# A threshold-attention and hardswish kernel on Trainium2: a different order of loads, warm-ups, biases and scores in its first microseconds, and a last tile in two halves

## The chip, the cores and the metric

The kernel runs on one core of one Trainium2 chip. The metric is the device time of one execution in microseconds (us). Only this core is used, so nothing is exchanged with other cores. In the tables, PE is the matmul engine, PEld its weight load, DVE the vector engine, ACT the scalar engine, POOL GpSimd, and SP the engine that issues most of the DMAs; a q behind a name stands for the engine's instruction queue.

## The reference, cut to what matters

The inputs are q, k and v of shape (8, 8, 576, 64), that is 8 batches of 8 heads, and the weights w_in (512 x 2048) and w_out (2048 x 512).

```python
scores = scale * np.matmul(q, k.transpose(0, 1, 3, 2))            # scale = 1/8
thresh = np.max(scores, axis=-1, keepdims=True) - tau             # tau = 0.02
scores = np.where(scores >= thresh, scores, -1000000000.0)
attn = softmax(scores)                       # with 1e-9 added to the sum
x = np.matmul(attn, v)                       # 4608 tokens x 512
h = x @ w_in
g = h * np.clip(h + 3.0, 0.0, 6.0) / 6.0
out = g @ w_out                              # 4608 x 512, float32
```

So each row of scores needs its maximum before anything else can be done to it. What lies under the maximum less tau is thrown away, the rest goes through a softmax, is multiplied by v, and the result of all heads goes through two large matmuls with a hardswish between them.

## The kernel before

**Work units.** A pair is two heads that share one tile of 128 rows: head a = 0 in rows 0 to 63, a = 1 in rows 64 to 127. A quad is two pairs, so there are 16 quads. A quad has 9 slots: 4 slots for each pair, of 128 queries each for both heads, and a ninth slot for the last 64 queries of both pairs. There are 144 slots. The main loop runs over them, with n as the slot's number. It is written for in-order engines: the order of the statements is the order on each engine, and no scheduler moves anything (`manual_schedule`).

**A slot's way.** `scores(n)` (L278) multiplies q and k on PE, in float32, into PSUM. A head's scores are 576 columns, more than a bank of 512, so each head takes two banks and two matmul calls, a wide and a narrow one. `sm_max` (L295) copies a head's scores to SBUF on DVE and takes the maximum in the same pass. `sm_bias` (L307) makes tau - scale * maximum on POOL. `sm_mask` (L310) on ACT adds that bias and blows up what is below zero; `sm_exp` (L315) on ACT takes the exponential and the sum. `sm_recip` (DVE) and `sm_norm` (POOL) normalise into bf16. Then the probabilities are transposed, by PE (`pe_transpose`, L336) or by a DMA from SP's queue (L333), and `av_main` and `av_rest` multiply them with v. `mm1`, `mm1_relu`, `mm1_gate` and `mm2_part` are the two large matmuls, from slot N1 = 22 on.

**Where the scores lie.** `score_col` (L275) puts head a = 1 in banks 0 and 1 and head a = 0 in banks 3 and 4, for every slot up to 24. Banks 2 and 5 take turns for transposes and products (`bank`), banks HB = 6 and OB = 7 serve the large matmuls later. At the start bank 6 holds the output of warm-ups, which nobody reads, and banks 6 and 7 hold the first transposes (`lead`).

**The lead-in.** `load_quad(0)` issues the loads of the first quad: `load_k(n)` and `load_q(n)` for pair n, two DMAs of 128 KB each, and `rest`, four DMAs of 32 KB for the last 64 keys (kr) and queries. SP issues them in the order k of pair 0, rest, k of pair 1, q of pair 1; the two DMAs for q of pair 0 are on ACT's queue. Meanwhile PE does `warm_up(17)`, transposes of an identity matrix that POOL makes first, so that PE is working when the data come. Then PE transposes the keys (L233) and, after 4 more warm-ups, the queries and kr (L461 to L466). ACT and DVE copy these out of PSUM (`evict`, L469 to L472), the first copy of keys on ACT since `copy_out` (L219) takes DVE for 0 <= now <= N1 and ACT otherwise. `scores(0)`, `sm_max`, `sm_bias` and `scores(1)` follow, and the loop begins. In slot n < N0 = 3 the loop does, in this order: the exponentials of slot n - 1 and the maxima and bias of slot n + 1, `sm_recip`, the masks of slot n, the transposes of `turns` with their copies, warm-ups, `scores(n + 2)` and six more warm-ups, `sm_norm`, and one or more loads. `turns` says which slot transposes which part of q and k: for quad 0, q of pair 1 in slot 1, k of pair 1 in slot 2, the rest of q in slot 3.

**The middle.** The rest of quad 3's k is transposed in slot 22 and copied at the start of slot 23 by `copy_out`, on ACT. For quads of batches 0 and 1 (quads 0 to 3) SP issues `rest`; for later quads POOL does, and k's part alone. Quad 4's is issued around slot 20.

**The end.** After the loop `rest2` works off what is left of the second matmul, in tiles of 128 tokens x 512 columns, 16 matmuls of 512 columns to a tile. `mm2_out` scales a tile on ACT or DVE into one of three buffers (osb), and `flush` sends it from SP. The very last tile (`last_out`, L656) is split: ACT evicts its left half and sends it on its own queue, DVE its right half, which SP sends.

Of the kernel before, what the change touches and what calls it, by code (L numbers as in the profile page):

```python
# [9 lines left out]
F32 = mybir.dt.float32  # L10
BF16 = mybir.dt.bfloat16
Ax = mybir.AxisListType
Alu = mybir.AluOpType
Act = mybir.ActivationFunctionType

P = 128
# [4 lines left out]
def kernel(  # L21
# [10 lines left out]
    nc = tc.nc  # L32
# [50 lines left out]
    def load_quad(quad):  # L83
        b, g = divmod(quad, 2)
        nat[quad] = (nat_pool.tile([P, 1152], F32, tag="nq", name="nq"),
                     nat_pool.tile([P, 4, 4, D], F32, tag="km", name="km"),
                     nat_pool.tile([P, 2 * D], F32, tag="kr", name="kr"))
        nq, km, kr = nat[quad]

        def main(dst, src, h, order, by=nc.sync):  # L90
            by.dma_start(out=dst[:, :, h, :], in_=src[b, 4 * g + h, 0:512, :].rearrange(order, t=4))

        def blocks_q(n, a, j):
            c = 32 * (2 * a + j)
            nc.sync.dma_start(out=nq[c:c + 32, n * S:(n + 1) * S].rearrange("p (k d) -> p k d", d=32),
                              in_=q[b, 4 * g + 2 * n + a, :, 32 * j:32 * j + 32].rearrange("(k r) d -> r k d", r=32))

        def blocks_k(n, a, j):
            c = 32 * (2 * a + j)
            nc.sync.dma_start(  # L100
                out=km[c:c + 32].rearrange("p t h d -> p (t h d)")[:, n * 512:(n + 1) * 512].rearrange(
                    "p (t m d) -> p t m d", t=4, d=32),
                in_=k[b, 4 * g + 2 * n + a, 0:512, 32 * j:32 * j + 32].rearrange("(m r t) d -> r t m d", r=32, t=4))

        def load_k(n):
            if b < NB:
                for a in range(2):
                    main(km, k, 2 * n + a, "(p t) d -> p t d")
            else:
                for a in range(2):  # L110
                    for j in range(2):
                        blocks_k(n, a, j)

        def load_q(n):
            if b < NB:
                for a in range(2):
                    main(nq[:, 0:1024].rearrange("p (t h d) -> p t h d", h=4, t=4), q, 2 * n + a, "(t p) d -> p t d",
                         by=nc.scalar if quad == n == 0 else nc.sync)
            else:
                for a in range(2):  # L120
                    for j in range(2):
                        blocks_q(n, a, j)

        def rest():
            for dst, src in ((kr[:], k), (nq[:, 1024:1152], q))[0:2 if b < NB else 1]:
                for n in range(2):
                    (nc.sync if b < NB else nc.gpsimd).dma_start(out=dst[64 * n:64 * n + 64, :].rearrange("p (h d) -> p h d", h=2),
                                      in_=src[b, 4 * g + 2 * n:4 * g + 2 * n + 2, 512:S, :].rearrange("h p d -> p h d"))

        def both():  # L130
            rest()
            load_k(1)

        if b < NB:
            loads.extend((lambda: load_k(0), lambda: load_q(0), rest, lambda: load_k(1), lambda: load_q(1)))
        else:
            loads.extend((lambda: load_q(0), lambda: load_k(0), lambda: load_q(1), both))
# [47 lines left out]
        for _ in range(count):  # L185
            nc.tensor.transpose(ps[:, HB, 0:P], identf[:], identf[:])

    warm_up(17)
    identb = singles.tile([P, P], BF16)
    nc.vector.tensor_copy(out=identb[:], in_=identf[:])  # L190
    three = singles.tile([P, 1], F32)
# [25 lines left out]


    def copy_out(out, in_):  # L219
        if 0 <= now <= N1:  # L220
            nc.vector.tensor_copy(out=out, in_=in_)
        else:
            nc.scalar.copy(out=out, in_=in_)  # L223
# [46 lines left out]
        return evict  # L270

    def first(n):
        return n > N1 + 2 and n % 2

    def score_col(n, a):  # L275
        return (704 if first(n) else 128) + (0 if a else 1536)

    def scores(n):  # L278
        quad, slot = divmod(n, NSLOT)
        w0 = 320 if first(n) else 384  # L280
        for k0, w in ((0, w0), (w0, S - w0)):
            for i in range(2 if slot == 8 else 1):
                for a in range(2):
                    pair = 2 * quad + (i if slot == 8 else slot // 4)
                    rows = slice(64 * i, 64 * i + 64) if slot == 8 else slice(0, P)
                    q0 = 512 if slot == 8 else slot % 4 * P
                    c0, kc = score_col(n, a) + k0, 64 * (1 - a) + k0
                    nc.tensor.matmul(ps_flat[rows, c0:c0 + w],  # L288
                                     qT_of(pair)[a * 64:(a + 1) * 64, q0:q0 + rows.stop - rows.start],
                                     kT_of(pair)[a * 64:(a + 1) * 64, kc:kc + w], start=True, stop=True)  # L290
# [4 lines left out]
    def sm_max(sl):  # L295
# [5 lines left out]
        for i in range(2):  # L301
            c0 = score_col(sl.n, i)
            nc.vector.tensor_scalar(out=sl.s[:, i, :], in0=ps_flat[:, c0:c0 + S],  # L303
                                    scalar1=1.0, scalar2=None, op0=Alu.mult, op1=Alu.max,
                                    accum_out=sl.m[:, i:i + 1])

    def sm_bias(sl):  # L307
        nc.gpsimd.tensor_scalar(out=sl.bias[:], in0=sl.m[:], scalar1=-scale, scalar2=tau, op0=Alu.mult, op1=Alu.add)  # L308

    def sm_mask(sl, i):  # L310
        s = sl.s[:, i, :]
# [142 lines left out]

    alloc_qk(0)
    evict = transpose_k(0)
    warm_up(4)
    lead = ps[:, HB:HB + 2, :]
    q_main = nat[0][0][:, 0:1024].rearrange("p (t h d) -> p t h d", h=4, t=4)
    q_rows = bank()  # L460
# [19 lines left out]
            queue.append(sl)  # L480
    scores(0)
    sm_max(queue[0])
    sm_bias(queue[0])
    scores(1)

    turns = {1: [("q", 1)], 2: [("k", 1)], 3: [("rest", 0)]}

    def turn_at(n, job, of):
        turns.setdefault(n, []).append((job, of))
# [41 lines left out]
    for n, sl in enumerate(queue):  # L531
# [18 lines left out]
        if n + 1 < len(queue):  # L550
            if n <= N1 or n > N2 + 1 or n % 2 == 0:
                sm_max(queue[n + 1])
            sm_bias(queue[n + 1])
        even = n >= N1 and n % 2 == 0
        if n >= N0:
            sm_recip(prev)
# [70 lines left out]
            evict = []  # L627
        for out_of_psum in evict:
            out_of_psum()
        if n == 0:  # L630
            warm_up(8)
        if n < N0:
            scores(n + 2)
            warm_up(6)
# [18 lines left out]
    count = [1, 0 if todo2 and todo2[0][2] else 1]  # L653


    def last_out():  # L656
        osb = o_pool.tile([P, d_model], F32, tag="osb", name="osb")
        r0, c = B * S - 64 - P, d_model // 2
        nc.scalar.activation(out=osb[:, 0:c], in_=o_ps[0][:, 0:c], func=Act.Copy, scale=1.0 / 6.0)
        nc.scalar.dma_start(out=out[r0:r0 + P, 0:c], in_=osb[:, 0:c])  # L660
        nc.vector.tensor_scalar_mul(out=osb[:, c:2 * c], in0=o_ps[0][:, c:2 * c], scalar1=1.0 / 6.0)
        nc.sync.dma_start(out=out[r0:r0 + P, c:2 * c], in_=osb[:, c:2 * c])

    def rest1(item, then, on_act=True):
        h = mm1(item, hb=(0, 1, 3, 4)[count[0] % 4])
# [4 lines left out]
    def rest2():  # L670
        while todo2:
            bb, mt, part = todo2.pop(0)
            mm2_part(bb, mt, part, ob=OB - count[1] % 2)
            if part == 3:
                flush()
                if (bb, mt) == (B // 2 - 1, 8):
                    last_out()
                else:
                    late.extend(mm2_out(bb, mt, on_act=(count[1] % 2 == 0)))
                count[1] += 1  # L680

    av_main(2 * last + 1, 0, 256)()
# [50 lines left out]
```

## Time and profile before

| what | value |
|---|---|
| time, median of 3 runs | 516.75 us (516.36 to 516.82) |
| profiled execution, span | 515.1 us |
| PE busy | 504.9 us (98%), 4127 matmuls |
| ACT busy | 451.8 us (88%) |
| DVE busy | 441.9 us (86%) |
| POOL busy | 300.4 us (58%) |
| chain of work that ended last, by engine | PE 79%, ACT 5%, DVE 2% |

The profile is of one execution. A busy time is the sum of an engine's own instructions; waiting and issuing aren't in it. PE's instructions overlap, and their ends are modelled, so a busy PE may still be waiting a little. The chain of work that ended last is followed back from the last instruction: at each step to what released it, or to the instruction before it on its engine. In a timeline, a row gives the start, the length, the instruction and, in brackets, how long the engine had stood before it and who ended that.

### The profile page before, as it was taken

The numbers are of one execution on the slowest core, as the hardware profiler recorded it, in microseconds if no ns is written. First come the engines' busy times: TensorE is split into PE (matmuls) and PEld (weight loads), VectorE is DVE, ScalarE is ACT, GpSimd is POOL, SyncE is SP. The second block draws the span as 40 slices with busy tenths as digits, with TensorE's granted clock in tenths as the row PEclk, the third lists the DMA queues.
The fourth block names the chain that finished last, engine by engine and source line by source line (L and its number), as shares of the span: only waits on it lengthen the run. The fifth ranks groups of instructions, "written<-read, shape, count | busy, mean of one in ns | idle before, by whom it ended". The sixth has DMA issues, their size and how long they took to land.

```text
span 515.1 us, 12094 instructions
## 1 busy us (share of the span) xinstructions
PE 504.9 (98%) x4127; PEld 318.6 (62%) x4127; DVE 441.9 (86%) x1124; ACT 451.8 (88%) x980; POOL 300.4 (58%) x538
## 2 busy tenths in 40 slices
PE   8999999999999999999999999999999999999997
PEld 6655566566655666666655666666655666667563
DVE  3698898998999999999999999999999999887260
ACT  3999989999999999999999999999999999986060
POOL 0788888756666666666566756657566655552000
PEclk9999999999999999999999999999999999999999
DMA  6998999989999999999898999999999997655132
GB/s 140 163 175 140 157 148 178 160 141 176 164 195 157 173 164 170 179 176 174 164 178 143 183 169 160 159 170 168 164 173 176 183 181 114 115 111 81 74 63 61
DMA packets 314094, 78.77 MB, mean 153 GB/s; under 512 B 296624, under 2 KB 309168, under 8 KB 314032
## 3 DMA queue, kind: packets, MB, share of 16 engines
q1 hardware_dynamic: 294464, 67.90, 79.8%
q0 software_dynamic: 18368, 9.71, 15.6%
q8 instruction: 32, 0.52, 0.4%
q10 hardware_dynamic: 1200, 0.39, 0.3%
q14 instruction: 30, 0.25, 0.2%
HBM read 36.70 MB, written 9.44 MB: 90 GB/s over the span
## 4 chain that ended last, share of the span: by engine, by line
PE 79%; ACT 5%; DVE 2%; issue 0%
PE ps L288 24%; PE ps L418 24%; PE ps L384 20%; PE ps L349 7%; PE ps L379 3%; ACT s L317 2%; ACT s L312 2%; PE ps L352 1%; ACT r L392 1%; DVE g L407 1%; DVE r L394 0%; PE ps L340 0%; DVE s L303 0%; ACT kT L223 0%; PE ps L258 0%
## 5 line engine op out<-in xcount | busy, mean ns | idle before, releaser
L325 POOL TENSOR_SCALAR pn<-s,rinv 128x576 bf16<-128x576 f32 x288 | 211.4, 746 | 18.9 <-issue 4.8
L303 DVE TENSOR_SCALAR_CACHE_REDUCE s<-ps 128x576 f32<-128x576 f32 x288 | 205.0, 748 | 16.4 <-PE ps L288 8.3
L312 ACT ACTIVATE s<-s,bias 128x576 f32<-128x576 f32 x288 | 205.8, 762 | 5.1 <-POOL bias L308 4.7
L317 ACT ACTIVATE s<-s 128x576 f32<-128x576 f32 x288 | 192.4, 670 | 0.3
L288 PE MATMUL ps<-kT,qT 64*128 64x384 f32 (+7 forms) x1280 | 175.4, 419 | 3.9 <-DVE s L303 2.4
L288 PEld LDWEIGHTS ps<-kT,qT 64*128 64x128 f32 (+1 forms) x1280 | 102.9, 175 | 60.3 <-issue 15.8
L418 PE MATMUL ps<-w_out_sb,g 128*128 128x512 bf16 x576 | 134.1, 379 | 0.0
L384 PE MATMUL ps<-xT,w_in_sb 128*128 128x256 bf16 x1024 | 130.9, 273 | 0.8 <-DVE g L407 0.8
L384 PEld LDWEIGHTS <-w_in_sb 128*128 128x128 bf16 x1024 | 95.6, 98 | 40.7 <-issue 21.7
L308 POOL TENSOR_SCALAR bias<-m 128x2 f32<-128x2 f32 x144 | 27.1, 188 | 150.5 <-DVE rinv L320 135.6
L407 DVE SCALAR_TENSOR_TENSOR g<-r,ps 128x512 bf16<-128x512 f32 x128 | 87.8, 687 | 15.0 <-ACT r L392 10.8
L418 PEld LDWEIGHTS <-g 128*128 128x128 bf16 x576 | 56.2, 98 | 56.8 <-issue 0.4
L392 ACT ACTIVATE r<-ps,three 128x512 f32<-128x512 f32 x81 | 55.5, 686 | 24.7 <-PE ps L384 20.5
L317 ACT ACTIVATION_READ_ACCUMULATOR s<-s 128x1 f32 x288 | 54.4, 189 | 0.0
L394 DVE TENSOR_SCALAR r<-ps 128x512 f32<-128x512 f32 x63 | 42.9, 680 | 0.0
L349 PE MATMUL ps<-pT,vm 128*64 128x256 bf16 (+1 forms) x480 | 39.1, 285 | 0.0
L349 PEld LDWEIGHTS <-vm 128*64 128x64 bf16 x736 | 27.2, 110 | 16.1 <-issue 14.6
L360 DVE CAST xT<-ps 128x256 bf16<-128x256 f32 (+1 forms) x60 | 26.2, 436 | 10.2 <-PE ps L352 10.2
L426 DVE TENSOR_SCALAR osb<-ps 128x512 f32<-128x512 f32 x31 | 20.9, 673 | 8.4 <-PE ps L418 8.4
L303 DVE DVE_READ_ACCUMULATOR s<-ps 128x1 f32 x288 | 23.8, 83 | 0.0
L320 DVE RECIPROCAL rinv<-rsum 128x2 f32<-128x2 f32 x144 | 23.0, 159 | 0.6 <-ACT s L317 0.6
L144 POOL DMA_DIRECT2D vm<-in_v_dram x28 | 21.5, 768 | 0.7 <-issue 0.6
(57 smaller groups left out, 253.9 us busy)
## 6 DMA issues: line engine op xcount, KB each, us to landing
out_dram<-osb SPq DMA_DIRECT2D x31, 256.0 KB, 2.7
nq<-in_q_dram SPq DMA_DIRECT2D x96, 72.0 KB, 3.4
km<-in_k_dram SPq DMA_DIRECT2D x96, 64.0 KB, 3.4
vm<-in_v_dram POOLq DMA_DIRECT2D x24, 128.0 KB, 4.3
km<-in_k_dram SPq DMA_DIRECT2D x16, 128.0 KB, 4.1
w_in_sb<-in_moe_w_in_dram POOLq DMA_DIRECT2D x16, 128.0 KB, 3.6
w_out_sb<-in_moe_w_out_dram POOLq DMA_DIRECT2D x16, 128.0 KB, 4.2
pT<-pn SPq DMA_TRANSPOSE x117, 4.0
```

What stands on the lines that cost most here:

```text
L288: nc.tensor.matmul(ps_flat[rows, c0:c0 + w], qT_of(pair)[a * 64:(a + 1) * 64, q0:q0 + rows.stop - rows.start], kT_of(pair)[a * 64:(a + 1) ...
L303: nc.vector.tensor_scalar(out=sl.s[:, i, :], in0=ps_flat[:, c0:c0 + S], scalar1=1.0, scalar2=None, op0=Alu.mult, op1=Alu.max, accum_out=sl ...
L308: nc.gpsimd.tensor_scalar(out=sl.bias[:], in0=sl.m[:], scalar1=-scale, scalar2=tau, op0=Alu.mult, op1=Alu.add)
L312: nc.scalar.activation(out=s, in_=s, func=Act.Prelu, bias=sl.bias[:, i:i + 1], scale=scale, alpha=REJECT)
L317: nc.scalar.activation(out=s, in_=s, func=Act.Exp, accum_out=sl.rsum[:, i:i + 1])
L325: nc.gpsimd.tensor_scalar(out=pn[:, i, :], in0=sl.s[:, i, :], scalar1=sl.rinv[:, i:i + 1], scalar2=1.0, op0=Alu.mult, op1=Alu.mult)
L349: nc.tensor.matmul(pb[a * 64:(a + 1) * 64, :], vm[:, 2 * hp + a, c * D:(c + 1) * D], pT[:, 5 * a + c, cols], start=(c == 0), stop=False)
L384: nc.tensor.matmul(ps[:, hb, n * 256:(n + 1) * 256], w_in_sb[:, ki, (ni + n) * P:(ni + n + 1) * P], xT[b][:, ki, c0:c0 + 256], start=(ki = ...
L392: nc.scalar.activation(out=r, in_=hps, func=Act.Relu, bias=three[:])
L394: nc.vector.tensor_scalar(out=r, in0=hps, scalar1=3.0, scalar2=0.0, op0=Alu.add, op1=Alu.max)
L407: nc.vector.scalar_tensor_tensor(out=out, in0=r, scalar=6.0, in1=hps, op0=Alu.min, op1=Alu.mult)
L418: nc.tensor.matmul(o_ps[0], gbuf[:, ni, mt * P:(mt + 1) * P], w_out_sb[:, ni, :], start=(ni == 0), stop=(ni == NI - 1))
```

## The change

- **Loads of quad 0.** `load_k(0)` goes on ACT's queue and `load_q(0)` on SP's, the other way round from before. kr of quad 0 goes on ACT's queue too.
- **`rest` of quad 4.** SP issues it, not POOL (SP up to quad 4, POOL from quad 5 on).
- **Warm-ups.** Instead of 17 transposes of the identity, PE does 2 matmuls of a constant zero, which needs no identity, and 14 transposes. The 4 warm-ups before the first transposes of queries and the 8 in slot 0 go.
- **A bias per head.** For slots 0, 1 and 2 the bias of each head is made by its own POOL instruction, right after its maximum, and not one for both after the second. ACT's mask of the first head needs the first alone.
- **Scores of slots 1 and 2.** They go head by head, not wide part by wide part. In slot 1 head 0 goes into banks 6 and 7, which no slot used before, and head 1 into banks 3 and 4, where slot 0 had its head 0. In slot 2 head 0 goes into banks 0 and 1 and head 1 into 3 and 4. Slot 0 and all from slot 3 on keep their places.
- **`turns`.** k of pair 1 is transposed and copied in slot 1, after its q, and not in slot 2.
- **`copy_out`.** DVE is taken up to slot N1 + 1 = 23, so that the two copies at the start of slot 23 move from ACT to DVE.
- **The last tile.** `last_tile` takes the place of `last_out`: 16 matmuls of the left 256 columns into bank 2, then 16 of the right 256 into bank 5. DVE evicts each half to its own osb buffer; ACT's queue sends the left one, SP the right one. `flush` comes before these matmuls.

```diff
--- before.py
+++ after.py
@@ -105,7 +105,7 @@
         def load_k(n):
             if b < NB:
                 for a in range(2):
-                    main(km, k, 2 * n + a, "(p t) d -> p t d")
+                    main(km, k, 2 * n + a, "(p t) d -> p t d", by=nc.scalar if quad == n == 0 else nc.sync)
             else:
                 for a in range(2):
                     for j in range(2):
@@ -114,8 +114,7 @@
         def load_q(n):
             if b < NB:
                 for a in range(2):
-                    main(nq[:, 0:1024].rearrange("p (t h d) -> p t h d", h=4, t=4), q, 2 * n + a, "(t p) d -> p t d",
-                         by=nc.scalar if quad == n == 0 else nc.sync)
+                    main(nq[:, 0:1024].rearrange("p (t h d) -> p t h d", h=4, t=4), q, 2 * n + a, "(t p) d -> p t d")
             else:
                 for a in range(2):
                     for j in range(2):
@@ -124,8 +123,9 @@
         def rest():
             for dst, src in ((kr[:], k), (nq[:, 1024:1152], q))[0:2 if b < NB else 1]:
                 for n in range(2):
-                    (nc.sync if b < NB else nc.gpsimd).dma_start(out=dst[64 * n:64 * n + 64, :].rearrange("p (h d) -> p h d", h=2),
-                                      in_=src[b, 4 * g + 2 * n:4 * g + 2 * n + 2, 512:S, :].rearrange("h p d -> p h d"))
+                    by = nc.scalar if quad == 0 and src is k else nc.sync if quad < 5 else nc.gpsimd
+                    by.dma_start(out=dst[64 * n:64 * n + 64, :].rearrange("p (h d) -> p h d", h=2),
+                                 in_=src[b, 4 * g + 2 * n:4 * g + 2 * n + 2, 512:S, :].rearrange("h p d -> p h d"))
 
         def both():
             rest()
@@ -185,7 +185,10 @@
         for _ in range(count):
             nc.tensor.transpose(ps[:, HB, 0:P], identf[:], identf[:])
 
-    warm_up(17)
+    blank = nc.const_aps.tensor(0.0, [P, P], F32)
+    for _ in range(2):
+        nc.tensor.matmul(ps[:, HB, 0:P], blank, blank, start=True, stop=True)
+    warm_up(14)
     identb = singles.tile([P, P], BF16)
     nc.vector.tensor_copy(out=identb[:], in_=identf[:])
     three = singles.tile([P, 1], F32)
@@ -217,7 +220,7 @@
 
 
     def copy_out(out, in_):
-        if 0 <= now <= N1:
+        if 0 <= now < N1 + 2:
             nc.vector.tensor_copy(out=out, in_=in_)
         else:
             nc.scalar.copy(out=out, in_=in_)
@@ -270,17 +273,21 @@
         return evict
 
     def first(n):
-        return n > N1 + 2 and n % 2
+        return n > N1 + 2 and n % 2 == 1
 
     def score_col(n, a):
+        if n in (1, 2):
+            return 1664 if a else 3200 if n == 1 else 128
         return (704 if first(n) else 128) + (0 if a else 1536)
 
     def scores(n):
         quad, slot = divmod(n, NSLOT)
         w0 = 320 if first(n) else 384
-        for k0, w in ((0, w0), (w0, S - w0)):
+        parts = ((0, w0), (w0, S - w0))
+        heads = range(2)
+        for group in [((a,), parts) for a in heads] if n in (1, 2) else [(heads, (part,)) for part in parts]:
             for i in range(2 if slot == 8 else 1):
-                for a in range(2):
+                for a, (k0, w) in [(a, part) for part in group[1] for a in group[0]]:
                     pair = 2 * quad + (i if slot == 8 else slot // 4)
                     rows = slice(64 * i, 64 * i + 64) if slot == 8 else slice(0, P)
                     q0 = 512 if slot == 8 else slot % 4 * P
@@ -303,9 +310,12 @@
             nc.vector.tensor_scalar(out=sl.s[:, i, :], in0=ps_flat[:, c0:c0 + S],
                                     scalar1=1.0, scalar2=None, op0=Alu.mult, op1=Alu.max,
                                     accum_out=sl.m[:, i:i + 1])
-
-    def sm_bias(sl):
-        nc.gpsimd.tensor_scalar(out=sl.bias[:], in0=sl.m[:], scalar1=-scale, scalar2=tau, op0=Alu.mult, op1=Alu.add)
+            if sl.n < N0:
+                sm_bias(sl, slice(i, i + 1))
+
+    def sm_bias(sl, of=slice(0, 2)):
+        nc.gpsimd.tensor_scalar(out=sl.bias[:, of], in0=sl.m[:, of], scalar1=-scale, scalar2=tau, op0=Alu.mult,
+                                op1=Alu.add)
 
     def sm_mask(sl, i):
         s = sl.s[:, i, :]
@@ -454,7 +464,6 @@
 
     alloc_qk(0)
     evict = transpose_k(0)
-    warm_up(4)
     lead = ps[:, HB:HB + 2, :]
     q_main = nat[0][0][:, 0:1024].rearrange("p (t h d) -> p t h d", h=4, t=4)
     q_rows = bank()
@@ -480,10 +489,9 @@
             queue.append(sl)
     scores(0)
     sm_max(queue[0])
-    sm_bias(queue[0])
     scores(1)
 
-    turns = {1: [("q", 1)], 2: [("k", 1)], 3: [("rest", 0)]}
+    turns = {1: [("q", 1), ("k", 1)], 3: [("rest", 0)]}
 
     def turn_at(n, job, of):
         turns.setdefault(n, []).append((job, of))
@@ -550,7 +558,8 @@
         if n + 1 < len(queue):
             if n <= N1 or n > N2 + 1 or n % 2 == 0:
                 sm_max(queue[n + 1])
-            sm_bias(queue[n + 1])
+            if n + 1 >= N0:
+                sm_bias(queue[n + 1])
         even = n >= N1 and n % 2 == 0
         if n >= N0:
             sm_recip(prev)
@@ -627,8 +636,6 @@
             evict = []
         for out_of_psum in evict:
             out_of_psum()
-        if n == 0:
-            warm_up(8)
         if n < N0:
             scores(n + 2)
             warm_up(6)
@@ -653,13 +660,16 @@
     count = [1, 0 if todo2 and todo2[0][2] else 1]
 
 
-    def last_out():
-        osb = o_pool.tile([P, d_model], F32, tag="osb", name="osb")
+    def last_tile(mt):
         r0, c = B * S - 64 - P, d_model // 2
-        nc.scalar.activation(out=osb[:, 0:c], in_=o_ps[0][:, 0:c], func=Act.Copy, scale=1.0 / 6.0)
-        nc.scalar.dma_start(out=out[r0:r0 + P, 0:c], in_=osb[:, 0:c])
-        nc.vector.tensor_scalar_mul(out=osb[:, c:2 * c], in0=o_ps[0][:, c:2 * c], scalar1=1.0 / 6.0)
-        nc.sync.dma_start(out=out[r0:r0 + P, c:2 * c], in_=osb[:, c:2 * c])
+        for half, by in enumerate((nc.scalar, nc.sync)):
+            o_half, columns = ps[:, (2, 5)[half], 0:c], slice(half * c, half * c + c)
+            for ni in range(NI):
+                nc.tensor.matmul(o_half, gbuf[:, ni, mt * P:(mt + 1) * P], w_out_sb[:, ni, columns],
+                                 start=(ni == 0), stop=(ni == NI - 1))
+            osb = o_pool.tile([P, d_model], F32, tag="osb", name="osb")
+            nc.vector.tensor_scalar_mul(out=osb[:, 0:c], in0=o_half, scalar1=1.0 / 6.0)
+            by.dma_start(out=out[r0:r0 + P, columns], in_=osb[:, 0:c])
 
     def rest1(item, then, on_act=True):
         h = mm1(item, hb=(0, 1, 3, 4)[count[0] % 4])
@@ -670,13 +680,15 @@
     def rest2():
         while todo2:
             bb, mt, part = todo2.pop(0)
+            if (bb, mt) == (B // 2 - 1, 8):
+                flush()
+                last_tile(mt)
+                todo2.clear()
+                continue
             mm2_part(bb, mt, part, ob=OB - count[1] % 2)
             if part == 3:
                 flush()
-                if (bb, mt) == (B // 2 - 1, 8):
-                    last_out()
-                else:
-                    late.extend(mm2_out(bb, mt, on_act=(count[1] % 2 == 0)))
+                late.extend(mm2_out(bb, mt, on_act=(count[1] % 2 == 0)))
                 count[1] += 1
 
     av_main(2 * last + 1, 0, 256)()
```

## The prediction

> **What bounds the kernel now.** I read the busy tenths and the chain of waits first, then the busy time in stretches, then the timelines of the first 24 us, of 69 to 88 us and of the last 5 us. Stretches (columns: stretch, length, busy us of PE, PEld, DVE, ACT, POOL with counts, clock, DMA share, GB/s):
> ```profile
> 24.00:65.00 41.00, 39.40 (x311) 23.67 (x311) 36.30 (x101) 40.55 (x91) 35.28 (x64) 1.00 0.98 158
> 107.00:470.00 363.00, 362.75 (x3085) 228.99 (x3084) 339.08 (x862) 340.99 (x749) 222.38 (x393) 1.00 1.04 162
> ```
> From 107 to 470 us PE never rests, so whatever the head saves before 107 us moves that whole block, unless PE has other work or a transfer to wait for. From 24 to 65 us ACT is busy 99%, with PE and DVE close behind. The timelines of ACT, DVE and PE at the start (start, length, what, idle time before it and who ended it):
> ```profile
> 10.44 1.44 ACT L312 ACTIVATE s<-s,bias 128x576 f32<-128x576 f32 x2 [3.33 <-POOL bias L308]
> ...
> 21.61 1.44 ACT L312 ACTIVATE s<-s,bias 128x576 f32<-128x576 f32 x2 [0.41 <-POOL bias L308]
> ```
> ```profile
> 8.67 0.76 DVE L303 TENSOR_SCALAR_CACHE_REDUCE s<-ps 128x576 f32<-128x576 f32 x1 [0.61 <-PE ps L288]
> ...
> 11.14 0.76 DVE L303 TENSOR_SCALAR_CACHE_REDUCE s<-ps 128x576 f32<-128x576 f32 x1 [1.02 <-PE ps L288]
> ...
> 19.84 0.76 DVE L303 TENSOR_SCALAR_CACHE_REDUCE s<-ps 128x576 f32<-128x576 f32 x1 [1.43 <-PE ps L288]
> ```
> ```profile
> 5.22 0.94 PE L233 MATMUL ps<-identf,km 128*128 128x128 f32 x4
> ...
> 7.40 1.33 PE L288 MATMUL ps<-kT,qT 64*128 64x384 f32 x8
> 9.49 1.91 PE L288 MATMUL ps<-kT,qT 64*128 64x384 f32 x8 [0.77 <-DVE s L303]
> 11.34 1.09 PE L186 MATMUL ps<-identf 128*128 128x128 f32 x8
> ...
> 18.47 1.24 PE L288 MATMUL ps<-kT,qT 64*128 64x384 f32 x8 [0.87 <-DVE kT L221]
> ```
> ACT begins at 10.44 us, after one serial line: keys land, PE transposes, ACT and DVE copy, scores, two maxima, bias. The scores of a slot wait for the maxima of the slot before (same banks), so DVE stands about 1 us per slot. Around slots 20 to 24 (69 to 88 us, all engines):
> ```profile
> 69.58 1.26 POOL L127 DMA_DIRECT2D kr<-in_k_dram  x2
> ...
> 71.70 1.44 ACT L312 ACTIVATE s<-s,bias 128x576 f32<-128x576 f32 x2 [0.70 <-POOL bias L308]
> ...
> 77.56 0.53 ACT L223 COPY kT<-ps 64x128 f32<-64x128 f32 x2 [0.95 <-DVE qT L266]
> ...
> 82.97 0.69 DVE L407 SCALAR_TENSOR_TENSOR g<-r,ps 128x512 bf16<-128x512 f32 x1 [0.71 <-ACT r L392]
> ...
> 84.37 1.03 PE L288 MATMUL ps<-kT,qT 64*128 64x256 f32 x4 [0.25 <-DVE qT L240]
> ...
> 86.70 0.66 PE L233 MATMUL ps<-identf,km 128*128 128x128 f32 x4 [0.32 <-DVE s L303]
> ```
> and the end of the chain in order of time:
> ```profile
> 500.88 10.38 PE ps L418 x48
> 511.25 0.02 issue
> 511.27 0.39 ACT osb L659
> 511.67 0.02 issue
> 511.69 0.42 DVE osb L661
> ```
> After the last matmul the two halves of one tile leave PSUM one after the other.
>
> **What the Trainium skill says.** "TensorE: Matmul & The Clock Gate", Part 1: PE runs at half clock until a free-running window of about 3.4 us has been busy, and falls back after an idle one. The trace agrees: transposes stand 0.2 us apart up to 5.8 us and 0.11 us apart after, 4.4 us after PE's first at 1.37 us. "DMA: Bandwidth & Descriptors", Issuing engines are not separate DMA queues: all issuers share the same 16 engines, and a second one saves only issue time. The trace's issue times: 0.45 us for one on ACT, 0.65 to 0.77 us on SP. "TensorEngine Tiling (Array Packing)", Key Properties: tiles on different rows work in parallel, so alternating the two heads of a slot may overlap. Here a slot's scores take 1.24 us when nothing is waited for and 1.91 us when the second head waits.
>
> **The change, part by part.** The sum is against the profiled span, 515.1 us; the runs shown have a median of 516.75 us (516.36 to 516.82), about 1.7 us above it, and I subtract the gain from that.
>
> 1. *Loads and warm-ups.* The transposes of the keys at 5.22 us follow the landing of the second key transfer at 5.08 us (issued by SP at 1.51). On ACT's queue the two query transfers of the same size, issued at 0.74 and 1.19, landed at 3.06 and 4.54; the keys take that place, so 0.54 us earlier. PE begins at about 0.8 us (DVE's first is at 0.87) rather than at 1.37, since the constant is set at 0.25; 16 warm-ups at 0.21 us from there, with a short wait for identf, end by 4.4 us: not the limit. The queries now land where the keys did, 5.1 us, or up to 0.3 us later, because kr (2 x 32 KB) goes beside them. With the 4 warm-ups gone (0.43 us), the 8 transposes that took 6.43 to 7.40 start at about 5.4: scores of slot 0 at 6.4 if PE is warm by then, 7.2 if it stays at half clock. Taken: 6.5, 0.9 us earlier; bounds 0.2 and 1.3. ACT's two extra DMAs (0.9 us) push its table load from 1.75 to 2.7, ending at 4.0, before its first copy (5.7 at the earliest). SP is past the first quad 1.3 us sooner, less what it waits on reused DMA semaphores; nothing reads those loads before 12 us.
> 2. *A bias per head* (slots 0 to 2). ACT began 0.33 us after the second maximum's end (10.11); now 0.33 after the first's (9.44): 0.67 us. POOL pays 3 x 0.19 us with 2 us idle around it. ACT starts at 10.44 - 0.9 - 0.67 = 8.87.
> 3. *Free banks, keys of pair 1 one slot sooner, 8 warm-ups less (1.09 us).* Half a slot's scores take 0.6 us (half of 1.24). Scores 0 end at 7.8, maxima 0 run 7.77 to 9.15. Slot 1: head 0 at 7.8 to 8.4 without a wait, head 1 at 8.55 to 9.15; maxima 1 at 9.15 to 10.5. Slot 2: head 0 at 9.25, head 1 at 10.6 to 11.2; maxima 2 end at 12.1. PE: 6 warm-ups, q and k of pair 1 (1.1 us) to 13.0, scores 3; maxima 3 begin at 14.3 (16.31 before). Scores 4 no longer wait 0.87 us on kT but on maximum 3, at 15.05; maxima 4 begin 1.74 us on, at 16.8 against 19.84: the DVE-PE loop is 3.0 us ahead. What was taken from the overlap of heads shows here as at most 2 x 0.67 us, hidden under DVE.
> ACT from 8.87 without a rest (2.67 us a slot) reaches slot 4 at 19.6 against 21.61: 2.0 ahead, having lost its 0.41 us wait. Its later short waits for the bias (0.08, 0.13, 0.11, 0.13, 0.24) then close too, so by slot 20 it is 2.0 + 0.7 = 2.7 ahead, within the loop's 3.0. I carry 2.7; bounds 1.8 (cold clock) and 3.5.
> 4. *kr of quad 4 from POOL to SP.* POOL loses 1.26 us that made bias 21 late (ACT's 0.70 us); but PE is busy without a break from 65 to 84 us, and ACT's next relu waits for PE: nothing. SP gains 1.3 us before DMA transposes that it holds from 73.7 us; their readers are products more than three slots away: nothing. Bounds for both: 0 to 0.3 gained.
> 5. *Slot 23's copies to DVE.* ACT is spared 0.95 + 0.53 us, DVE gets 0.55 us into waits of 0.49 and 0.71 us. DVE's gate at 82.97 then starts at 82.4, PE's waits at 84.37 and 86.70 (0.25 and 0.32 us) close, and ACT keeps ahead: 0.5 us. Bounds: 0 and 1.4, all of PE's idle time from 77 to 107 us.
> 6. *The last tile.* 32 matmuls of 256 columns at 0.109 us (L384: 8 in 0.87) for 16 at 0.216: +0.03. Its first half is evicted and sent under the second half's matmuls; after the last matmul stand one 0.42 us eviction and SP's DMA, as before; ACT's 0.39 + 0.03 us are gone: 0.4. Bounds 0.2 and 0.6.
>
> Sum: 2.7 + 0.5 + 0.4 = 3.6 us: span 511.5, time 516.75 - 3.6 = 513.15.
>
> **The rivals.**
> *The lead is absorbed* (0.12): the loop of slots 5 to 21 meets something that hasn't moved. For it: the DMA engines' share is about 1 from 24 us on, and the DMA transposes take 4 to 6 us. Against: no long wait in the list of waits names a load. It would leave the tail's 0.4 and about 1.2: 515.2.
> *Keys land no earlier* (0.15): the engines are shared, and the queries, now second, set the scores at 7.2. Gain 1.8 + 0.5 + 0.4: 514.05.
> *PE's clock falls* (0.06), the one that ends slower: 13 warm-ups are gone, and if the windows between 6 and 24 us aren't busy enough, each of 3.4 us does half its work, 1.7 us lost. It decides from the third window on (3 x 1.7 = 5.1 against 3.6): 518.3. Against: PE's longest rest here is 0.87 us before, and step 3 shortens rests.
> *As worked out* (0.67): 511.8 to 514.4.
>
> **How the numbers follow.** Predicted 513.15. Low: the high bounds of steps 1 to 3 and half of 5's, 3.5 + 1.0 + 0.4 = 4.9: 511.85. High: up to the absorbed case, 515.2; beyond lie the worse half of that case (0.06) and the clock (0.06). Within 0.2% (1.03 us, about what a measurement tells from no change) lie that half, down to the tail's 0.4 alone, and a clock lost for just two windows (0.01): 0.07. Slower: 0.05. Faster: the rest, 0.88.
>
> **What would show it.** Key transposes at about 4.65 us, scores 0 at 6.5, ACT's first mask at 8.9 without a later gap over 0.2 us up to slot 20; maximum 4 near 16.8; PE's block at 107 us starting near 103.8; no ACT eviction after the last matmul. Wrong if transposes stay 0.2 us apart after 7 us, if ACT's 20th mask is less than 2 us early, or if PE shows new waits on DMAs between 20 and 107 us.

## The result, and the profile after

| | before | after |
|---|---|---|
| time, median of 3 runs | 516.75 us (516.36 to 516.82) | 513.41 us (512.79 to 513.46) |
| ratio to before | | 0.9934, 95% interval 0.9911 to 0.9956 |
| again, on one chip with other kernels | 516.92 us | 513.03 us, ratio 0.9926 (0.9913 to 0.9938) |
| span of the profiled execution | 515.1 us | 511.0 us |

The change makes the kernel faster by 3.3 to 3.9 us. The two profiled executions differ by 4.05 us in their spans: the one of before took 516.88 us, a little more than its three timed ones, and the one of after was the shortest of its three. In this section times are counted from the start of each profiled execution, and the lead is how much sooner the same instruction starts after the change than before it. Among the experiments, two kernels are compared by times counted from slot 0's maxima, unless the text says otherwise.

The busy time in the two stretches that the prediction shows, taken 2.7 and 3.2 us earlier (same columns):
```profile
21.30:62.30 41.00, 39.65 (x320) 23.89 (x316) 36.31 (x102) 40.75 (x92) 35.37 (x65) 1.00 1.05 159
103.80:466.80 363.00, 362.80 (x3087) 229.35 (x3087) 339.41 (x862) 341.06 (x748) 221.61 (x393) 1.00 0.99 162
```
The block of 363 us in which PE never rests is the same as before. It starts 3.35 us sooner, as the chain of work that ended last shows, before and after:
```profile
107.15 1.03 PE ps L384 x8
```
```profile
103.80 1.03 PE ps L394 x8
```
So the gain is the 3.35 us saved ahead of this block, 0.11 us more by PE's last matmul, and 0.58 us in the tail. The timeline of ACT at the start, and its next wait:
```profile
3.51 1.28 ACT L226 ACT_TABLE_LOAD   x1 [3.51 <-issue]
...
9.26 1.44 ACT L322 ACTIVATE s<-s,bias 128x576 f32<-128x576 f32 x2 [2.53 <-POOL bias L317]
```
After 9.26 us ACT has no wait over 0.03 us until one of 0.12 us at 38.8 us. It started 1.18 us sooner than before, and its wait of 0.41 us at slot 4 is gone. DVE and PE:
```profile
8.18 0.76 DVE L310 TENSOR_SCALAR_CACHE_REDUCE s<-ps 128x576 f32<-128x576 f32 x1 [0.53 <-PE ps L295]
...
12.36 0.76 DVE L310 TENSOR_SCALAR_CACHE_REDUCE s<-ps 128x576 f32<-128x576 f32 x1 [0.65 <-PE ps L295]
...
17.77 0.76 DVE L310 TENSOR_SCALAR_CACHE_REDUCE s<-ps 128x576 f32<-128x576 f32 x1 [1.04 <-POOL pn L335]
```
```profile
1.77 3.19 PE L186 MATMUL ps<-identf 128*128 128x128 f32 x14
5.32 0.63 PE L236 MATMUL ps<-identf,km 128*128 128x128 f32 x4 [0.36 <-DMA km<-in_k_dram]
...
6.90 4.00 PE L295 MATMUL ps<-kT,qT 64*128 64x384 f32 x20
11.09 1.23 PE L295 MATMUL ps<-kT,qT 64*128 64x384 f32 x4 [0.18 <-DVE s L310]
12.26 0.87 PE L186 MATMUL ps<-identf 128*128 128x128 f32 x6
```
The scores of slots 0 to 2 now run nearly without a rest, from 6.90 to 12.26 us. But PE still waits for keys (0.36 us before 5.32), later than before. Maxima 4 begin at 17.77 against 19.84, 2.08 us ahead, and this 2.08 stays to the hundredth for every maximum up to slot 24. Around slot 23:
```profile
71.85 1.44 ACT L322 ACTIVATE s<-s,bias 128x576 f32<-128x576 f32 x2 [0.27 <-POOL bias L317]
...
73.84 0.69 ACT L402 ACTIVATE r<-ps,three 128x512 f32<-128x512 f32 x1 [0.55 <-PE ps L394]
...
75.37 0.58 DVE L224 COPY kT<-ps 64x128 f32<-64x128 f32 x2
...
79.26 1.44 ACT L322 ACTIVATE s<-s,bias 128x576 f32<-128x576 f32 x2 [0.17 <-POOL bias L317]
...
84.01 0.65 PE L236 MATMUL ps<-identf,km 128*128 128x128 f32 x4 [0.32 <-DVE s L310]
```
ACT, which had to wait 0.95 us here and then copy, now waits 0.55 us for PE and otherwise only shortly for the bias. The work hasn't gone: the chain of work that ended last ran over ACT's copies before, and now runs over DVE's, on DVE as far as 90.4 us and on ACT after that. Before and after:
```profile
77.56 0.26 ACT kT L223
...
78.12 1.44 ACT s L317 x4
```
```profile
75.45 0.19 DVE kT L224
...
77.51 1.44 DVE s L310 x4
...
90.43 0.86 ACT s L327 x3
```
DVE is now busy 11.93 of the 12 us from 78 to 90, against 10.61 before. The lead grows from 2.08 us to 3.35 us at slot 31 and 3.44 us at slot 40 (ACT's mask 40 at 126.49 us against 129.92). The end of the chain:
```profile
504.28 3.51 PE ps L668 x32
507.79 0.02 issue
507.81 0.42 DVE osb L671
```

### The profile page after: what moved, and what is told of

Same layout as the page of the kernel before. It is cut to its first block, busy times and chain, and to the rows that moved or that the text cites. A ratio compares the mean times of both kernels' runs of the same rounds, so it can differ in the third digit from the quotient of the medians.

```text
span 511.0 us, 12107 instructions
## 1 busy us (share of the span) xinstructions
PE 503.4 (99%) x4132; PEld 319.8 (63%) x4132; DVE 442.8 (87%) x1127; ACT 450.3 (88%) x977; POOL 298.6 (58%) x539
## 4 chain that ended last, share of the span: by engine, by line
PE 80%; DVE 4%; ACT 3%; issue 1%; DVEq 0%
PE ps L295 24%; PE ps L428 23%; PE ps L394 20%; PE ps L359 7%; PE ps L389 3%; DVE s L310 1%; PE ps L362 1%; ACT s L327 1%; ACT s L322 1%; DVE g L417 1%; DVE r L404 1%; PE ps L668 1%; ACT r L402 1%; PE ps L350 0%; DVE xT L370 0%
## 5 line engine op out<-in xcount | busy, mean ns | idle before, releaser
L428 PE MATMUL ps<-w_out_sb,g 128*128 128x512 bf16 x560 | 130.7, 379 | 0.0
L317 POOL TENSOR_SCALAR bias<-m 128x2 f32<-128x2 f32 (+1 forms) x147 | 27.5, 187 | 148.4 <-DVE rinv L330 132.1
L428 PEld LDWEIGHTS <-g 128*128 128x128 bf16 x560 | 54.6, 98 | 55.0 <-issue 0.4
```

The lines of the kernel that those rows point to most:

```text
L317: nc.gpsimd.tensor_scalar(out=sl.bias[:, of], in0=sl.m[:, of], scalar1=-scale, scalar2=tau, op0=Alu.mult, op1=Alu.add)
L428: nc.tensor.matmul(o_ps[0], gbuf[:, ni, mt * P:(mt + 1) * P], w_out_sb[:, ni, :], start=(ni == 0), stop=(ni == NI - 1))
```

## The experiments

Theory A: up to slot 21 the loop of PE and DVE (scores, maxima, scores) sets the pace and ACT runs within it; at slots 23 to 30 ACT is the limit; after that PE is. What is saved counts only where the limit is. The rival: everything saved in the head adds up. The first kernels undo one part of the change each.

**Loads on their old queues.**
```diff
-main(km, k, ..., by=nc.scalar if quad == n == 0 else nc.sync)
+main(km, k, ...)
-main(nq..., q, ...)
+main(nq..., q, ..., by=nc.scalar if quad == n == 0 else nc.sync)
-by = nc.scalar if quad == 0 and src is k else nc.sync if quad < 5 else nc.gpsimd
+by = nc.sync if quad < 5 else nc.gpsimd
```


> The changed kernel with quad 0's loads on their old queues (keys and kr on SP, queries on ACT). In the changed kernel the keys' second transfer landed at 5.19 us and slot 0's scores began at 6.90. Theory A (the queue swap brought the keys no earlier; what moved the scores was the 4 warm-ups that went): keys land at 5.0 to 5.2, scores of slot 0 begin within 0.15 us of 6.9, the end moves by under 0.2 us. Rival (the swap carries the 0.5 us): scores at about 7.4, every later maximum 0.5 us later, the end 0.5 us later.

Measured: 512.64 us (512.59 to 513.1), ratio 0.9921 (0.9909 to 0.9933). The keys landed at 5.00 us. PE's timeline:
```profile
5.14 0.64 PE L237 MATMUL ps<-identf,km 128*128 128x128 f32 x4 [0.18 <-DMA km<-in_k_dram]
...
6.58 2.75 PE L296 MATMUL ps<-kT,qT 64*128 64x384 f32 x13
```
The scores begin at 6.58, not later than in the changed kernel but 0.3 us sooner, so the expected 0.15 us was missed on the good side. The queue swap gave nothing; whether it costs time is not settled by the times, since the intervals overlap. The landings say more: in the four profiles with the old queues here (the kernel before, this one and the two last experiments) the keys' second transfer landed at 4.82 to 5.08 us, in the ten with the new queues at 5.02 to 5.49. So the swap brings the keys a little later, not sooner. Why is open.

**One bias for both heads.**
```diff
-            if sl.n < N0:
-                sm_bias(sl, slice(i, i + 1))
...
-            if n + 1 >= N0:
-                sm_bias(queue[n + 1])
+            sm_bias(queue[n + 1])
```
and `sm_bias(queue[0])` after the first maxima, as before.

> The changed kernel with one bias instruction for both heads in slots 0 to 2. In the changed kernel ACT's first mask is at 9.26 us and ACT then rests only 0.12, 0.13, 0.24 and 0.27 us up to slot 23, waiting for maxima. Theory A (from slot 4 to 21 the DVE-PE loop is what counts, and ACT runs within it): the first mask 0.67 us later, ACT that much late up to slot 11, then its short waits close and it is at most 0.1 us late at slot 21; the end moves by 0 to 0.15 us. Rival (each saved wait adds up, as the prediction's step 2 has it): 0.67 us late all the way, the end 0.67 us later.

Measured: 512.84 us (512.6 to 514.88; ratio 0.993, 0.9917 to 0.9943). ACT's first mask and its next waits:
```profile
9.71 1.44 ACT L320 ACTIVATE s<-s,bias 128x576 f32<-128x576 f32 x2 [3.16 <-POOL bias L315]
```
```profile
63.27 1.44 ACT L320 ACTIVATE s<-s,bias 128x576 f32<-128x576 f32 x2 [0.17 <-POOL bias L315]
...
71.64 1.44 ACT L320 ACTIVATE s<-s,bias 128x576 f32<-128x576 f32 x2 [0.27 <-POOL bias L315]
```
Counted from slot 0's maxima the first mask is 0.68 us late. The waits of 0.12 and 0.13 us are gone and that of 0.24 has shrunk to 0.17; at maxima 40 the kernel is 0.02 us behind the changed one, at PE's end 0.05. The bias per head is worth 0.68 us at its place and nothing at the end.

**Old banks for slots 1 and 2.**
```diff
 def score_col(n, a):
-    if n in (1, 2):
-        return 1664 if a else 3200 if n == 1 else 128
...
-for group in [((a,), parts) for a in heads] if n in (1, 2) else [(heads, (part,)) for part in parts]:
+for group in [(heads, (part,)) for part in parts]:
```


> The changed kernel with the scores of slots 1 and 2 in the old banks and order, the 8 warm-ups of slot 0 still gone. Theory A (the loop counts): maxima of slots 1 and 2 about 1 and 2 us later, maxima 3 about 1.0 us later (16.2 against 15.2), all later maxima up to slot 21 and the end 0.8 to 1.1 us later. Rival (slot 3 and later wait for the copies of pair 1 and for the warm-ups in any case): maxima 3 within 0.2 us, the end too.

Measured: 514.11 us (ratio 0.9955, 0.9939 to 0.9971), but the profiled execution took 516.8 us, with maxima 3 at 19.19 us: PE had run at half pace around 14 us. It was run once more:

> The kernel of e3_banks_back once more, since PE's matmuls ran at half pace for some 3 us around slot 2 in its profiled execution. Theory A (that was the clock falling back in one execution; the banks themselves cost 0.8 to 1.1 us): maxima 3 at about 1.0 us after the changed kernel's counted from the scores of slot 0, the median near 514.1 us again. Rival (the banks' own wait lets the clock fall each time): half pace again, maxima 3 near 19 us.

Measured: 22 executions in two groups: 13 from 513.75 to 514.89 us, 9 from 516.63 to 517.21 us; the ratio over all is 0.9969 (0.9958 to 0.9981). The profiled one is of the second group (stretches; PE's granted clock is the third number from the end):
```profile
8.00:12.00 4.00, 2.88 (x14) 1.45 (x11) 2.69 (x7) 2.62 (x6) 0.57 (x3) 1.00 0.69 156
12.00:16.00 4.00, 4.00 (x15) 2.91 (x14) 1.72 (x7) 3.78 (x10) 1.72 (x5) 0.50 0.70 136
16.00:20.00 4.00, 4.00 (x23) 2.97 (x21) 1.89 (x3) 1.82 (x5) 1.98 (x3) 0.65 0.59 80
```
and PE's timeline there:
```profile
9.12 1.91 PE L293 MATMUL ps<-kT,qT 64*128 64x384 f32 x8 [0.57 <-DVE s L308]
11.58 2.96 PE L293 MATMUL ps<-kT,qT 64*128 64x384 f32 x8 [0.55 <-DVE s L308]
14.47 1.54 PE L186 MATMUL ps<-identf 128*128 128x128 f32 x6
```
PE rested 1.1 of 4 us between 8 and 12 us, and its clock then was at half for 6.8 us, to 18.8 us: six transposes took 1.54 us and not 0.87. All nine of the second group have a mean granted clock of 0.993 and the thirteen others 0.999 or 1.000, so this fall is what divides the groups (6.8 of 515 us at half take 0.7% off the mean). It cost about 2.8 us. In the others the old banks cost some 1.2 us (the middle one took 514.19 us) against the changed kernel's 513.03 us on the same chip, a little over theory A's figure; but no profile of such an execution was taken, so where that 1.2 us lies is inferred, not shown. Neither theory was wholly right: the clock falls in two executions of five. Why in these is open. In the profile here and in that of the first run, PE was busy 68 and 67% of the 3.4 us just before the fall, with no rest over 0.58 us. In the kernel with the keys of pair 1 in slot 2, further down, it was busy no more than that, 68% of the 3.4 us from 17.74 to 21.15, with a rest of 0.95 us, and the clock stayed at 1.00. So neither that share nor the longest rest decides alone. The free-running window that the prediction cites would account for it; no run tests that.

**Slot 23's copies on ACT.**
```diff
-        if 0 <= now < N1 + 2:
+        if 0 <= now <= N1:
```


> The changed kernel with the two copies of slot 23 on ACT again. The changed kernel's lead grew from 2.08 us at slot 21 to 3.44 us at slot 40. Theory A (the copies on DVE carry most of that): the lead stays at 2.1 to 2.6 us, the end 0.8 to 1.3 us later. Rival (POOL's freed DMA issues carry it): the lead still reaches 3.2 us or more, the end moves by under 0.25 us.

Measured: 514.41 us (ratio 0.9952, 0.9939 to 0.9965). ACT's timeline has the old wait again:
```profile
74.01 0.69 ACT L402 ACTIVATE r<-ps,three 128x512 f32<-128x512 f32 x1 [0.55 <-PE ps L394]
75.66 0.53 ACT L226 COPY kT<-ps 64x128 f32<-64x128 f32 x2 [0.95 <-DVE qT L269]
```
Maxima 40 come 1.41 us later than in the changed kernel. That is all the growth of the lead from 2.08 to 3.44 us, so it is this one condition; the chain of work that ended last runs over ACT's copies again. PE's end is 1.72 us later: the last 0.3 us arise near 497 us, where ACT waits 0.98 us and not 0.53, and have no part in this.

**kr of quad 4 from POOL.**
```diff
-... else nc.sync if quad < 5 else nc.gpsimd
+... else nc.sync if quad < 4 else nc.gpsimd
```


> The changed kernel with kr of quad 4 issued by POOL again. Theory A (step 4 of the prediction: PE is busy without a break there, so POOL's 1.26 us cost nothing): mask 22 about 0.7 us later, the lead at slot 40 within 0.25 us of the changed kernel's 3.44, the end too. Rival (this is what made the lead grow from 2.08 to 3.44 us at slots 22 to 30): the lead stays 0.7 us or more smaller, the end 0.7 us or more later.

Measured: 513.19 us (ratio 0.9929, 0.9916 to 0.9941). The wait that this DMA issue made is there, and costs nothing:
```profile
68.13 1.26 POOL L127 DMA_DIRECT2D kr<-in_k_dram  x2
...
70.26 1.44 ACT L322 ACTIVATE s<-s,bias 128x576 f32<-128x576 f32 x2 [0.70 <-POOL bias L317]
```
Mask 22 is 0.8 us later, maxima 40 by 0.01 us.

**The old last tile**, `last_out` in place of `last_tile`.
```diff
-            if (bb, mt) == (B // 2 - 1, 8):
-                flush()
-                last_tile(mt)
-                todo2.clear()
-                continue
...
+                if (bb, mt) == (B // 2 - 1, 8):
+                    last_out()
```


> The changed kernel with the old last tile (one tile of 512 columns, its halves evicted by ACT and DVE one after the other). Theory A: from PE's last matmul to the end of the span 3.81 us as before, against 3.2 in the changed kernel, the end 0.4 to 0.6 us later. Rival (the last transfers' landing hides the eviction): under 0.2 us.

Measured: 513.5 us (ratio 0.9937, 0.9926 to 0.9949). From PE's end to the end of the span it took 3.66 us, against 3.24 in the changed kernel and 3.82 before. The two evictions stand one after the other again:
```profile
507.74 0.38 ACT L666 ACTIVATE osb<-ps 128x256 f32<-128x256 f32 x1 [2.86 <-PE ps L428]
...
508.16 0.42 DVE L668 TENSOR_SCALAR osb<-ps 128x256 f32<-128x256 f32 x1 [6.63 <-ACT osb L666]
```
In eleven of the twelve profiles with the new tail that stretch is 3.22 to 3.24 us long, in one 3.36. The new tail is worth 0.42 us.

**Old warm-ups**: 17 transposes at the start, 4 ahead of the queries, 8 in slot 0.
```diff
-    blank = nc.const_aps.tensor(0.0, [P, P], F32)
-    for _ in range(2):
-        nc.tensor.matmul(ps[:, HB, 0:P], blank, blank, start=True, stop=True)
-    warm_up(14)
+    warm_up(17)
...
     evict = transpose_k(0)
+    warm_up(4)
...
+        if n == 0:
+            warm_up(8)
```


> The changed kernel with the old warm-ups: 17 transposes of the identity at the start, 4 ahead of the queries, 8 in slot 0. Theory A (warm-ups stand in PE's order, and in the head PE's order is the loop): scores of slot 0 begin 0.4 to 0.5 us later, maxima 3 and all up to slot 21 0.9 to 1.4 us later, the end about 1.1 us later. Rival (they fill time in which PE would wait for DVE anyway): maxima 3 within 0.5 us, the end too.

Measured: 513.61 us (ratio 0.9941, 0.9929 to 0.9953). Counted from the start of the execution, scores of slot 0 begin at 7.20 us, 0.30 later, maxima 3 at 15.80, 0.59 later, and everything to slot 40 0.60 later. Counted from slot 0's maxima, 0.30 us are left from maxima 3 on. These are the 8 warm-ups of slot 0: maxima 2 come 1.70 us later, and most of that is made up by maxima 3. The 0.30 ahead of slot 0's maxima lie within what this start differs by from one execution to the next (see the changed kernel again). So the mechanism is theory A's, at a third to a half of the size expected.

**Keys of pair 1 in slot 2.**
```diff
-    turns = {1: [("q", 1), ("k", 1)], 3: [("rest", 0)]}
+    turns = {1: [("q", 1)], 2: [("k", 1)], 3: [("rest", 0)]}
```


> The changed kernel with the keys of pair 1 transposed and copied in slot 2 again. Theory A (the loop counts): maxima 3 0.5 us earlier, since PE has 4 transposes less before the scores of slot 3, but the scores of slot 4 wait for the copy, so maxima 4 0.4 to 0.9 us later and everything after it, the end 0.4 to 0.9 us later. Rival (the transposes cost the same in either slot): the end within 0.2 us.

Measured: 513.69 us (513.28 to 515.41; ratio 0.9945, 0.9933 to 0.9957). From slot 0's maxima, maxima 3 come 0.44 us sooner and maxima 4 0.54 us later, and 0.55 us is what is left at slot 40. The profiled execution was the longest, 515.41 us. There PE's transposes still stood 0.21 us apart at 7.6 us, and slot 0's maxima began at 10.19 us, 2.0 us later than in the changed kernel:
```profile
7.57 0.84 PE L475 MATMUL ps<-identf 128*128 128x128 f32 x3
8.35 4.58 PE L295 MATMUL ps<-kT,qT 64*128 64x384 f32 x20
```

**The changed kernel again.**


> The changed kernel unaltered, for a comparison on one chip. Theory A (an execution's time moves by when PE's clock rises and whether it falls back): its times spread over 512.6 to 514 us, scores of slot 0 between 6.6 and 7.6 us, and everything from slot 4 to 40 in step with that start. Rival (the spread comes later): the start in place, the later part moved.

Measured: 513.03 us (512.73 to 513.65). In its profile slot 0's maxima are 0.13 us later than in the first one and maxima 40 by 0.13 too: the difference is made before 8 us. In the nine profiles of kernels with this head (this one, the first, and the experiments that alter only what follows slot 0's maxima) slot 0's maxima began at 7.95 to 8.82 us, and once at 10.19. One profile of each kernel can't resolve a few tenths of a microsecond there. The single times of 514.4 to 515.4 us among those of the joint bias, the old warm-ups and the keys in slot 2 would fit a late start; only one of these executions was profiled, the one with 10.19 us.

**Fewer warm-ups.** If the loop is the limit, warm-ups in PE's order ahead of work that the loop waits for can go: the six of slot 0 and the six of slot 3. With the old load queues as well, as in the first experiment:
```diff
             scores(n + 2)
-            warm_up(6)
+            if n:
+                warm_up(6)
...
-            if n in (3, 6):
+            if n == 6:
```


> The changed kernel with the loads on their old queues and without the six warm-ups of slot 0 and the six of slot 3, which stand in PE's order ahead of transposes and scores that the DVE-PE loop waits for. Theory A (up to slot 21 the loop is what counts, and from slot 21 PE): maxima 3 0.6 to 0.7 us earlier counted from the scores of slot 0, maxima 6 about 1.1 us earlier, ACT's waits of 0.12, 0.13 and 0.24 us gone, the lead at slot 40 and the end 0.9 to 1.2 us better than with the loads alone put back (512.64 us). Rival 1 (ACT is the limit from its first mask on): 0.5 us at most. Rival 2 (PE's clock needs them): transposes 0.2 us apart for some 3 us after 7 us, the time 1 to 3 us longer in some executions.

Measured: 511.73 us (511.42 to 512.07), ratio 0.9899 (0.9886 to 0.9911). Counted from slot 0's maxima, maxima 3 are 0.66 us and all from slot 11 to 40 are 1.0 us ahead of the loads alone put back. ACT has no wait left between its first mask and slot 23. Rival 1 falls: up to slot 21 ACT was not the limit.

And without the three identity transposes ahead of slot 0's scores:
```diff
-    for _ in range(3):
-        nc.tensor.transpose(q_rows[:, 0:P], identf[:], identf[:])
```


> As e9_less_warm, and the three identity transposes ahead of the scores of slot 0 go too. Theory A: scores of slot 0 begin about 0.2 to 0.3 us earlier, when ACT has copied the keys, and all later maxima and the end with them by 0.1 to 0.25 us. Rival (the second head's scores wait for DVE's copy of kr, which ends after those transposes in any case): under 0.1 us. If the clock needs them: as in rival 2 of e9_less_warm, more often.

Measured: 511.47 us (511.35 to 511.52), ratio 0.9893 (0.988 to 0.9906), the fastest here: 1.56 us less than the changed kernel on the same chip. PE:
```profile
6.43 4.21 PE L296 MATMUL ps<-kT,qT 64*128 64x384 f32 x20
10.82 1.23 PE L296 MATMUL ps<-kT,qT 64*128 64x384 f32 x4 [0.18 <-DVE s L311]
11.98 0.66 PE L237 MATMUL ps<-identf,nq 128*128 128x128 f32 x4
```
The 0.26 us between this and the kernel before it are not separated by the intervals. In the four timed executions of each the clock did not fall (its mean was 0.999 or 1.000): in the profiles, with scores in free banks, PE has no rest over 0.2 us from the scores of slot 0 to 28 us.

## Why the prediction was right, and where its sum was not

The forecast was 513.15 us, the result 513.41. Direction and place were right: a shorter line ahead of a PE-bound block, slot 23, the tail. The mechanism was right but for the loads and the bias. That the sum is so close is luck: it came out by errors of opposite sign. In the profiled executions 2.08 + 1.4 + 0.58, together the 4.05 us, stand where I had 2.7 + 0.5 + 0.4. At the low end of the range, half of step 5's bound of 1.4 is 0.7 and not the 1.0 put in; the result lies inside either way.

1. *Step 1, 0.9 us: 0.50 between the two profiles, and for another reason.* "The keys take that place" failed. The four large transfers landed at 3.06, 3.96, 4.54 and 5.08 us before and at 3.06, 3.94, 4.54 and 5.18 after, queries first, keys second and fourth, whichever queue each was on. I took the issue time for the engine's: 0.45 us on ACT. It belongs to the transfer: the first key DMA held ACT's queue for 0.70 us (SP's for 0.77 before) and the first query DMA SP's for 0.51 (ACT's for 0.45 before). So the keys' second issue still came at 1.45 us. This was the rival "keys land no earlier", with a milder price because PE's clock was up by 5.3 us. The trace agrees with what the prediction quoted of the Trainium skill ("DMA: Bandwidth & Descriptors", Issuing engines are not separate DMA queues); I had not drawn the conclusion. Read off PE's two timelines, the 0.50 us between the scores' starts (7.40 and 6.90) are 0.43 for the 4 warm-ups that went and 0.31 for the four transposes of the keys, which ran at full pace, less 0.10 because the keys came later and 0.14 for the transposes of queries and kr. The 0.31 is when the clock rose, by 5.3 and not 5.8 us, and that differs between executions of the same head as well, so these profiles can't tell whether the change brought it.
2. *Step 2, 0.67 us: measured 0.68 at the first mask, nothing at the end.* ACT's lead of 2.7 us was the wrong number to carry. The loop's was the smaller one, 2.08, and ACT's own lead, 1.18 us at its first mask, reaches it by slot 20 with or without the early bias.
3. *Step 3, 3.0 us: measured 2.08.* 0.4 came from step 1. The other 0.5 is "half a slot's scores take 0.6 us". A head alone takes 0.97 to 1.17 us (slot 1's first head from 7.98 to 8.95), since the 1.24 us for both are two heads side by side. The Trainium skill ("TensorEngine Tiling (Array Packing)", Key Properties) says that different tiles can run in parallel, and I had cited it; head by head that parallelism is gone. Slots 1 and 2 ended at 12.26 us, not 11.2, and DVE waited 0.65 us for them: it was not hidden under DVE. Of the 2.08 us, 0.50 is there at slot 0's maxima and 1.58 comes after. Undone one at a time, the keys' earlier turn is worth 0.55 of this 1.58 and the 8 warm-ups 0.30. The old banks cost 1.2 us in the executions whose clock didn't fall, more than the 0.7 that is left, so the parts don't simply add; no profile separates them.
4. *Step 4, nothing: confirmed*, the 0.7 us of ACT's wait included.
5. *Step 5, 0.5 us: measured 1.4*, at the end of my bounds. I followed the one gate at 82.97 and PE's next two waits. But in the profile of before ACT was busy 11.95 of the 12 us from 78 to 90, and the chain ran over it: it was the limit there, and what it was spared (0.95 + 0.53 us) counts almost in full. The bound of 1.4 was right by luck, for PE's waits did not close. Between slot 23 and the block they add up to 1.43 us before and 1.16 after; of the two that I named, the one of 0.25 us closed and the one of 0.32 still stands (at 84.01). Most of the 1.3 us saved there shows in PE's busy time, 29.72 before and 28.73 after for the same 235 instructions; that fits a PE that counts as busy while it waits a little, but no run isolates it.
6. *Step 6, 0.4 us: 0.42 by the experiment*, 0.58 between the two profiles. The old tail took 3.82 us in one profile and 3.66 in the other, and those 0.16 lie after the last DMA was issued.

The rival of the falling clock was real, though not for this change. With the same missing warm-ups but the old banks it struck 9 executions of 22 and cost 2.8 us. I had put 1.7 us for each window of 3.4 us; the clock was at half for 6.8 us, two of them. The change takes away the warm-ups, but fills PE's rests with scores from free banks. The Trainium skill ("TensorE: Matmul & The Clock Gate", Part 1) has the clock fall after an idle window, and tells of a kernel in which short rests between groups of matmuls made it fall; here PE was not idle but 72% busy in the 4 us before.

## What to carry to other kernels

When several engines run close to their limit one after the other, find for each stretch which of them has no rest: time saved there counts almost in full, as at slot 23 (1.4 of 1.48 us), and time saved on an engine that only follows is given back, as with the bias per head (0.68 us at its place, nothing at the end). Then look which engine the work was moved to, since that one may be the next limit, as DVE was here. Moving a load to another queue brought it no earlier here, and its issue time of 0.70 us went along with it. Warm-up work is worth its place only where the engine would otherwise rest; in front of work that others wait for it can cost nearly its full length: six transposes of 0.71 us cost 0.66 in slot 0, eight others there 0.30.

## What the runs showed of the hardware that was not expected

- PE's clock fell to half after a stretch in which PE was busy 2.88 of 4 us, in 9 of 22 executions of one program. In both profiles of it the clock stayed at half for 6.8 us (12.0 to 18.8 and 11.5 to 18.3 us), though PE was busy all the while.
- When the clock first rises varies from one execution to the next with the same start of the program: transposes were at full pace by 5.3 us in one and still at half at 7.6 us in another, with PE at work since 0.78 us in both. Slot 0's maxima came 2.0 us later there, 0.3 of it because the keys' transposes began later. The profile's clock column gives 1.00 in both; it's the pace of the transposes that tells.
- Four transfers of 128 KB on two queues landed in the same order and within 0.1 us of the same times with keys and queries swapped between the queues, in the profiles before and after the change.
